# Channel mixes of the full final steps placed later in the following step, and the second row block's cast placed earlier

## The chip, the cores and the metric

The kernel runs on one core of a Trainium2 chip. The metric is the device time of one launch in microseconds (us), median of several runs; the kernel before takes 1473.58 us (six runs, 1470.38 to 1484.61). TensorE (PE) multiplies matrices into PSUM; VectorE (DVE) and ScalarE (ACT) read PSUM and work elementwise; GpSimd (POOL) adds in SBUF and issues part of the DMAs; SyncE (SP) only issues DMAs. Every engine works through its own instructions in order and waits on semaphores for the others.

## The reference

```python
# _attn_ref: a causal 7-tap filter per head along the sequence
w = softmax(weight)                            # 8 heads x 7 taps
x = out.reshape(B, S, D)                       # (8, 4224, 192), sum of 7 shifted rows
# _moe_ref
theta = x @ w_theta
zr, zi = x * cos(theta), x * sin(theta)
yr = einsum('ts,bsd->btd', w_tok_r, zr)        # 4224 x 4224 token mix
yi = einsum('ts,bsd->btd', w_tok_i, zi)
u = x + yr + yi
return u + maximum(u @ w_ch, 0.0)              # channel mix
```

Nearly all the work is the two token mixes, with matrices of 4224 x 4224 each applied to 8 x 192 = 1536 columns. After them each row of u goes through a 192 x 192 channel mix, is clipped at zero and added to u.

## The kernel before, in words

The 4224 tokens are cut into 33 chunks of 128 on the side that is summed over, and 33 row blocks of 128 on the output side. A chunk's filtered x, its cosine and sine products and their sums and differences are the seven planes of a `z` tile; at most 11 chunks are in SBUF at a time (`NW`). Output row blocks are visited in pairs, 17 visits to a round, and chunks come and go in a rolling manner, so that the whole run is 58 steps (`NSTEP`). Each step (`class Step`) takes a pair of row blocks through all chunks that are active, and adds the result to the partial sums of these rows, which live in DRAM (`part`) between visits. The tiles with the partial sums are called `pv`, two to a step, of 128 x 1536 float32.

A step of a pair has seven runs (`runs`), each over the n active chunks with two matmuls of 128 x 384 for each chunk (`mix`, L427): products of the two row blocks are shared so that seven runs do the work of eight. After a run `give` evicts an accumulator: DVE adds it to `pv` (L392). With n = 11, a full step, that is 154 matmuls.

The steps t = 41 to 57 are final: their rows are complete after them. Those from 41 to 52 have 11 chunks and a pair of rows; these are the "full final steps" that the change touches. From t = 53 (`late`) n falls to 9, 7, 6, 4 and 2, and their outputs go another way, with transposes on TensorE (`turn_u`).

For each of the two row blocks i of a full final step, `outputs` (L474) schedules this:

- `cast(i, g)` for g = 0, 1: ACT makes a float16 copy `ub` of half of `pv` (L449).
- `cross_u(i)`: ACT issues a DMA that transposes `ub` through the crossbar into `uT` (L155); `uT` has two buffers.
- `output(i, g)` for g = 0, 1: TensorE multiplies `uT` by the channel weights `wch` in 8 matmuls (`channel_mix`, L138), DVE clips and adds in one instruction (L464), and SP writes 384 KB to DRAM (L469).

The order of the work is written out by hand. Each of these tasks has a due time in us after the end of its own step, on a clock where a matmul counts 0.324 us per chunk and run (`self.time`, 24.95 for a full step). `step_events` turns the due time into a position in the following step, from 0 to 7 runs:

```python
found.append((7 * begin / steps[t].time, f))
```

and `mix` emits the task ahead of the first chunk whose place, run r plus c/n, has reached that position. TensorE, DVE, ACT and POOL then execute in the order of emission (`in_order`); for SP's DMAs the tile framework decides. Other tasks of a step that share these queues: `w_tasks` (DVE turns and sums the next step's weight tiles, L327 and L339), `load_w` (POOL loads weights into `st`, L314), `load_rows` (SP loads the next step's `pv`, L363; six buffers, and the transfer waits for the output transfers of the buffer's last user), and `add_x` (L370), which adds x to the partial sums of rows that have not had it. `add_x` has two forms. POOL adds an `xr` tile, which SP loads (L373 and L374); or, for late steps and four steps ahead, POOL issues DMAs that accumulate x into `part` in DRAM (L379), which happens in the steps from t = 49 on.

Of the kernel before, what the change touches and what calls it, by code (L numbers as in the profile page):

```python
# [16 lines left out]
def kernel(  # L17
# [262 lines left out]
    class Step:  # L280
# [193 lines left out]
        def outputs(self):  # L474

            found = []
            for i in range(len(self.tbs)):
                if not self.late:
                    at = (4 if i else 0.9 - self.time / 7) if self.pair else 0.7
                    for g in range(NG):  # L480
                        found.append((at + g, lambda i=i, g=g: self.cast(i, g)))
                        found.append((at + 10.5 + 2.8 * g,
                                      lambda i=i, g=g: self.output(i, g)))
                    found.append((at + 2, lambda i=i: self.cross_u(i)))
                    continue
                at = 1.2 if i or not self.pair else 0.6 - self.time / 7
                every, turn, mix = 2.0, 1.2, 3.6
                for g in range(NG):
                    found.append((at, lambda i=i, g=g: self.cast(i, g)))
                    found.append((at + turn, lambda i=i, g=g: self.turn_u(i, g)))  # L490
                    found.append((at + mix, lambda i=i, g=g: self.output(i, g)))
                    at += every
            return found
# [202 lines left out]
    for at, f in sorted(outputs, key=lambda e: e[0]):  # L696
        if at >= sum(s.time for s in steps):
            f()
# [28 lines left out]
```

## Time and profile before

| what | us |
|---|---|
| median of six runs | 1473.58 |
| lowest, highest | 1470.38, 1484.61 |
| the profiled execution | 1476.82 |
| its span, first to last instruction | 1475.0 |
| PE busy | 1419.9 (96%) |
| DVE busy | 1015.4 (69%) |
| POOL busy | 435.7 (30%) |
| ACT busy | 323.1 (22%) |
| crossbar transfers uT<-ub, 24 of them: issue to landing, least, median, most | 3.2, 6.9, 29.5 |

How to read it: the rows of the trace name the line, engine and operation, then what is written and read (`v<-wch,uT` reads `wch` and `uT` and writes `v`). In the rows of waits stand total time, count and the longest. In the chain and the time line the first two numbers are start and duration. An `x8` counts merged instructions. In rows of a window stand the busy times of PE, weight loads (PEld), DVE, ACT and POOL with counts, the clock that TensorE was granted, the share of the DMA engines, and GB/s.

### The profile page before, as it was taken

What the parts mean: (1) busy time and instruction counts of PE and PEld (TensorE: products, weight loads), DVE (VectorE), ACT (ScalarE), POOL (GpSimd) and SP (SyncE); (2) the same over time, 40 slices, a digit from 0 to 9 for tenths busy, and PEclk for the clock granted to TensorE, in tenths of its full rate; (3) what the DMA queues carried; (4) which work ended last, traced back from release to release, by engine and by line L of the source; (5) the groups of instructions that cost most, each with busy time, mean ns of one, the idle gap of its engine ahead of it and who ended that gap; (6) DMA issues with size and microseconds to landing.
All of it is one profiled execution on the core that took longest, in us unless ns stands there. A gap on an engine that the chain in (4) does not pass through costs nothing.

```text
span 1475.0 us, 23773 instructions
## 1 busy us (share of the span) xinstructions
PE 1419.9 (96%) x9807; PEld 886.9 (60%) x9807; DVE 1015.4 (69%) x1050; ACT 323.1 (22%) x413; POOL 435.7 (30%) x655
## 2 busy tenths in 40 slices
PE   7889999999999999999999999999999999995997
PEld 4556666666666666666656566666666666663665
DVE  6884554555458687777767758769787786773675
ACT  6861111111134353000000005245001001000034
POOL 7422211111223322522413333342133133333210
PEclk9999999999999999999999999999999999997999
DMA  9976756464699999997978799999889989999983
GB/s 178 223 162 145 143 100 147 95 151 89 157 223 221 221 215 270 193 241 172 243 168 210 173 196 238 192 238 263 154 199 212 210 196 234 197 272 140 225 220 119
DMA packets 272028, 281.98 MB, mean 191 GB/s; under 512 B 106672, under 2 KB 240176, under 8 KB 271920
## 3 DMA queue, kind: packets, MB, share of 16 engines
q0 software_dynamic: 162464, 92.15, 47.7%
q1 hardware_dynamic: 71824, 178.88, 34.9%
q10 hardware_dynamic: 37632, 9.44, 5.0%
q8 instruction: 77, 1.26, 0.3%
q14 instruction: 31, 0.25, 0.1%
HBM read 245.49 MB, written 108.13 MB: 240 GB/s over the span
## 4 chain that ended last, share of the span: by engine, by line
PE 85%; DVE 6%; DMA 4%; ACT 3%; issue 1%; POOL 0%; DVEq 0%; ACTq 0%; SPq 0%
PE y L427 77%; PE v L138 5%; DMA uT<-ub 3%; PE pc L200 2%; DVE pv L392 1%; ACT z L240 1%; PE tp L160 1%; DVE wt L339 1%; DVE wt L327 1%; DVE z L251 1%; DVE z L245 1%; ACT uT L148 1%; DVE pv L464 1%; DMA xw<-xw 1%; ACT pv L390 0%
## 5 line engine op out<-in xcount | busy, mean ns | idle before, releaser
L427 PE MATMUL y<-z,wt 128*128 128x384 f16 x7656 | 1291.5, 327 | 12.2 <-DVE pv L392 11.2
L427 PEld LDWEIGHTS <-wt 128*128 128x128 f16 x7656 | 740.5, 98 | 488.1 <-issue 14.7
L392 DVE TENSOR_TENSOR pv<-y,pv 128x768 f32<-128x768 f32 x324 | 308.5, 953 | 311.3 <-PE y L427 271.8
L327 DVE STREAM_TRANSPOSE wt<-st 128x1408 f16<-128x1408 f16 (+7 forms) x224 | 327.7, 1465 | 40.0 <-PE y L427 36.2
L314 POOL DMA_DIRECT2D st<-in_moe_w_tok_i_dram x232 | 132.7, 579 | 509.0 <-DVE wt L327 494.6
L314 POOL DMA_DIRECT2D st<-in_moe_w_tok_r_dram x232 | 132.8, 579 | 453.8 <-DVE wt L327 440.5
L339 DVE TENSOR_TENSOR wt<-wt 128x1408 f16<-128x1408 f16 (+7 forms) x216 | 217.3, 1006 | 45.7 <-PE y L427 43.7
L148 ACT ACTIVATE z<-pc 128x768 f16<-128x768 f32 x65 | 52.9, 813 | 389.6 <-PE pc L200 389.6
L449 ACT ACTIVATE ub<-pv 128x768 f16<-128x768 f32 x66 | 52.5, 836 | 361.7 <-DVE pv L392 350.8
L138 PEld LDWEIGHTS <-uT 128*128 128x128 f16 x1056 | 91.5, 98 | 41.9 <-DMA uT<-ub 18.4
L390 ACT ACTIVATE pv<-y 128x768 f32<-128x768 f32 x66 | 53.7, 813 | 282.7 <-PE y L427 282.7
L464 DVE SCALAR_TENSOR_TENSOR pv<-v,pv 128x768 f32<-128x768 f32 x66 | 62.6, 951 | 34.1 <-PE v L138 32.2
L187 POOL DMA_DIRECT2D xw<-in_x_dram x132 | 76.3, 584 | 30.5 <-DMA xw<-xw 7.5
L374 POOL TENSOR_TENSOR pv<-pv,xr 128x1536 f32<-128x1536 f32 x24 | 74.7, 3113 | 10.1 <-issue 8.8
L148 ACT ACTIVATE uT<-tp 128x768 f16<-128x768 f16 x79 | 63.0, 815 | 63.0 <-PE tp L160 62.1
L251 DVE TENSOR_TENSOR z<-z 128x768 f16<-128x768 f16 x132 | 73.3, 556 | 3.8
L138 PE MATMUL v<-wch,uT 128*128 128x192 f16 x528 | 54.9, 248 | 18.7 <-DMA uT<-ub 16.8
L240 ACT ACTIVATE z<-v,half_pi 128x768 f16<-128x768 f32 x66 | 59.6, 902 | 42.9 <-PE v L138 42.7
L245 DVE TENSOR_TENSOR z<-z 128x1536 f16<-128x1536 f16 x66 | 60.3, 949 | 9.9 <-ACT z L240 9.9
L138 PE MATMUL v<-wth,uT 128*128 128x192 f16 x528 | 55.0, 248 | 3.0 <-ACT z L240 2.8
L240 ACT ACTIVATE z<-v 128x768 f16<-128x768 f32 x66 | 53.1, 805 | 0.0
L160 PE MATMUL tp<-ident,z 128*128 128x128 f16 x396 | 33.0, 220 | 8.5 <-ACT z L240 8.0
(43 smaller groups left out, 146.8 us busy)
## 6 DMA issues: line engine op xcount, KB each, us to landing
part<-pv SPq DMA_DIRECT2D x79, 768.0 KB, 4.1
pv<-part SPq DMA_DIRECT2D x79, 768.0 KB, 5.8
out_dram<-pv SPq DMA_DIRECT2D x66, 384.0 KB, 5.3
st<-in_moe_w_tok_r_dram POOLq DMA_DIRECT2D x136, 176.0 KB, 5.2
st<-in_moe_w_tok_i_dram POOLq DMA_DIRECT2D x136, 176.0 KB, 5.2
xs<-z SPq DMA_DIRECT2D x132, 96.0 KB, 4.6
xw<-in_x_dram POOLq DMA_DIRECT2D x121, 96.0 KB, 6.0
xr<-xs SPq DMA_DIRECT2D x24, 384.0 KB, 4.5
```

Of the source, the lines that this page charges most:

```text
L138: pe(nc.tensor.matmul(v[:, k, b * D : (b + 1) * D], lhsT=tT[:, 3 * k + b + i, :], rhs=w[:, 2 * b + i, :], start=(i == 0), stop=(i == 1),))
L148: act(nc.scalar.activation(out=out, in_=in_, func=AT.Copy))
L187: nc.gpsimd.dma_start(out=self.xw[lo : lo + n, h, :, :], in_=x[:, t0 : t0 + n, :].rearrange("b s d -> s b d"),)
L240: act(nc.scalar.activation(**args))
L245: dve(nc.vector.tensor_tensor(out=o, in0=xv, in1=o, op=ALU.mult))
L251: dve(nc.vector.tensor_tensor(out=z[:, o, :], in0=z[:, a, :], in1=z[:, b, :], op=ALU.subtract))
L314: pool(nc.gpsimd.dma_start(out=st[a * Q : (a + 1) * Q, 0:nb, :, 0:n] .rearrange("i r bt s -> i (r bt) s"), in_=w[self.tbs[0] * P : (self.t ...
L327: dve(nc.vector.transpose(self.w[name][:, 0 : self.n, :, :], self.st[int(name[1])][:, int(name[0]) - 1, :, 0 : self.n * Q] .rearrange("p b ...
L339: dve(nc.vector.tensor_tensor(out=self.w[name][:, 0 : self.n, :, :], in0=self.w[a][:, 0 : self.n, :, :], in1=self.w[b][:, 0 : self.n, :, : ...
L392: dve(nc.vector.tensor_tensor(out=o, in0=yv, in1=o, op=ALU.add))
L427: pe(nc.tensor.matmul(y[cn][:, q, 0:BH], lhsT=self.w[wn][:, c, :, :].rearrange("p bt i -> p (bt i)"), rhs=chunks[k].z[:, zn, q * BH : (q + ...
L464: dve(nc.vector.scalar_tensor_tensor(out=ub, in0=channel_mix(self.uT[i][:, 6 * g : 6 * g + 6, :], wch), scalar=0.0, in1=ub, op0=ALU.max, o ...
```

## The change

Three due times in `outputs` change, for full final steps alone. The casts of the second row block (i = 1) are due 1 and 2 us after the step's end instead of 4 and 5, and its crossing at 3 instead of 6. The first row block's casts and crossing keep theirs (-2.66, -1.66 and -0.66). The four outputs no longer follow the casts by a fixed distance: they are due at 12, 14.7, 17.5 and 20.2 us after the step's end, instead of 7.84, 10.64, 14.5 and 17.3. What is computed stays the same, and each engine has the same instructions as before. On ACT and POOL their order stays the same as well; on PE, DVE and SP it changes.

```diff
             for i in range(len(self.tbs)):
                 if not self.late:
-                    at = (4 if i else 0.9 - self.time / 7) if self.pair else 0.7
+                    at = 1 if i or not self.pair else 0.9 - self.time / 7
                     for g in range(NG):
                         found.append((at + g, lambda i=i, g=g: self.cast(i, g)))
-                        found.append((at + 10.5 + 2.8 * g,
+                        found.append((12 + 5.5 * i + 2.7 * g,
                                       lambda i=i, g=g: self.output(i, g)))
                     found.append((at + 2, lambda i=i: self.cross_u(i)))
                     continue
```

## The prediction

> **What bounds the kernel now.** I read the page first (shares, chain), then TensorE's waits inside the full final steps, then the chain and the time line around the longest of them. Times are us of the one profiled execution.
>
> ```profile
> span 1475.0 us, 23773 instructions
> PE 1419.9 (96%) x9807; PEld 886.9 (60%) x9807; DVE 1015.4 (69%) x1050; ACT 323.1 (22%) x413; POOL 435.7 (30%) x655
> PE 85%; DVE 6%; DMA 4%; ACT 3%; issue 1%; POOL 0%; DVEq 0%; ACTq 0%; SPq 0%
> ```
>
> TensorE is busy 96% of the span, so 55 us of idle time is all that any reordering can win. The change touches t = 41 to 52, about 1050 to 1400 us, and there TensorE's waits are these:
>
> ```profile
> PE v L138 <- DMA uT<-ub: 16.8, 3, 14.8
> PE y L427 <- DVE pv L392: 0.7, 2, 0.4
> ```
>
> Three waits for a crossbar transfer (a "crossing") hold nearly everything, one of them 14.8 us. The chain of waits shows where each begins and how long its crossing was under way:
>
> ```profile
> 1276.38 10.26 DMA uT<-ub
> 1286.68 0.83 PE v L138 x8
> ...
> 1305.46 9.81 DMA uT<-ub
> 1315.31 0.83 PE v L138 x8
> ...
> 1334.09 23.77 DMA uT<-ub
> 1357.90 1.46 PE v L138 x8
> 1359.37 4.83 PE y L427 x16
> ```
>
> The second column is the duration. Each of the three is the first row block's crossing of a step (t = 49, 50, 51), wanted by the first channel mix of the next step. After the third, the eight channel-mix matmuls take 1.46 instead of 0.83 and the next 16 take 4.83 instead of 2.60 (that row elsewhere in the chain): the idle time also lowered the clock, for 0.6 + 2.2 = 2.9 us. What went on in the long wait:
>
> ```profile
> 1333.89 1.75 POOL L379 DMA_DIRECT2D part<-xs  x2
> 1334.09 1.32 ACTq L155 DMA_TRANSPOSE uT<-ub  x1
> 1337.33 0.34 SPq L363 DMA_DIRECT2D pv<-part  x1
> 1337.66 17.81 ACTq L155 DMA_TRANSPOSE uT<-ub  x1
> ```
> ```profile
> 1334.00:1343.00 9.00, 9.00 (x57) 5.28 (x54) 5.22 (x5) 1.63 (x3) 3.40 (x5) 1.00 1.30 220
> 1343.00:1358.00 15.00, 0.25 (x2) 0.10 (x2) 0.89 (x2) 0.00 (x0) 2.33 (x4) 0.62 1.25 72
> ```
>
> An accumulating transfer from POOL, the crossing and a partial-sum load from SP started together. The last three numbers of the lower rows are granted clock, DMA share and GB/s: while the DMA engines stay fully occupied (1.25), the rate falls from 220 to 72 GB/s and the clock to 0.62. In the steps before t = 49 there are no accumulating transfers, and no crossing was waited for.
>
> **The change, part by part.**
>
> *Channel mixes later.* A full step is 154 token matmuls of about 0.1625 us (96 in 15.60 in the chain). The emission positions 2.20, 2.985, 4.07 and 4.85 runs become 3.37, 4.12, 4.91 and 5.67, rounded up to the next of a run's 11 chunks: 50, 66, 90 and 108 matmuls ahead of the four mixes become 76, 92, 110 and 126. So they move by 26, 26, 20 and 18 matmuls: 4.2, 4.2, 3.25 and 2.9 us. Work is neither added nor removed. At t = 48 the first crossing was issued at 1248.72 and its mix began at 1257.57: 8.85 us of cover, which becomes 13.1. The second (1252.30 to 1265.39) had 13.1 and gets 16.3. If crossings land as they did:
> - waits of 1.29 (crossing 10.26) and 0.79 (9.81) go entirely: 2.1;
> - the 14.75 us wait shrinks by 4.2 to 10.5; it is still long enough to lose the clock, so the 2.9 stays;
> - the second crossing of that step was issued at 1337.66 and, at its 29.5 us (the longest landing of a crossing), landed at 1367.2. After a resume at 1357.9 come mix 1.46, 16 matmuls 4.83, mix 0.66, 18 matmuls 2.92, so the third mix wants it at 1367.8: just covered.
>
> *DVE.* Each moved output takes its 0.95 us DVE pass along. In steps where POOL adds x, S3 is held up (4.59 us at 1314.46 instead of 0.88, beside POOL's 3.12 us add at 1315.18), and in the chain an output pass and a 1.55 us weight turn then stood ahead of the eviction for which TensorE waited (the 0.7 above; about 0.3 more at 1098). Now the output pass leaves that place (-0.95) and TensorE arrives one mix (0.66) earlier: 0.29 better in each. I take 0.6 for all of them, between 0 and 1.0. Later in the step DVE has the passes that it no longer has earlier; every eviction has a whole run, 3.6 us, before its accumulator is written again, and I count at most two passes (1.9) ahead of one. Cost 0.
>
> *Second block's cast.* The order of ACT's instructions does not change, and neither does POOL's. ACT has nothing else in these steps: its waits there were
>
> ```profile
> ACT ub L449 <- DVE pv L392: 308.8, 20, 40.3
> ```
>
> so the cast starts when the eviction is done, wherever it stands. At 1332.48 and 1336.05 the two casts are already 3.57 us apart, one run, not the 6.66 of the old positions. Gain 0, from 0 to 0.3; its crossing does not start earlier either.
>
> *SP's queue.* A step's four output transfers stay four; each moves with its mix, and behind each pair of them stands a partial-sum load that waits for them to land (the buffer is theirs). So the loads come up to about 4 us later too; one load of x stands between two outputs now. The first load of a pair is over 30 us ahead of its use (issued at 1269.01, for the step that starts near 1306); the tightest I find, at 1408.49 for a step that starts near 1423 and wants it two runs in, has some 13. POOL's x add waits for such a load as well and has over 10. Cost 0, from 0 to 1.
>
> *Last full step.* t = 52's outputs run in a step of 9 chunks, where the last comes after the final matmul. Near the end TensorE has short waits for output passes (0.46, 0.43); one more DVE pass there costs 0 to 0.95; I take 0.3.
>
> Sum: 2.1 + 4.2 + 0.6 - 0.3 = 6.6 off this execution. It ran 1476.82 with a span of 1475.0 (1.8 around it) and is 3.2 above the median 1473.58. Without its crossing waits (16.8 + 2.9) it would have taken some 1457, and the fastest run shown is 1470.38, so every run seems to hold 13 us or more of them. Where they lie in more than one place, each place gives up to 4.2: from 6.6 (one long wait) to 13 (three). I take 8, nearer to the row that I have: 1473.6 - 8 = **1465.5**.
>
> [...] The crossings landed after 3.2 to 29.5 us, median 6.9. [...]
>
> **Rivals.**
> 1. *The long crossing does not come back* (0.22). The partial-sum load at 1337.33 sat between the two crossings; behind later outputs it moves to about 1341. If that load was what choked them, the whole 14.75 + 2.9 + 2.1 + 0.6 = 20.3 goes: 1476.8 - 20.3, about 1456. Against: the accumulating transfers and the crossing still start together, since both hang on DVE's order.
> 2. *Hidden or eaten* (0.15): later outputs lengthen the crossing by the 4.2 us given: 1473, with 1470 to 1478.
> 3. *Slower* (0.18): outputs and the first load of the pair now run right ahead of the crossing, in company with accumulating transfers. If the crossings at the ends of t = 49 and 50 take the 23.8 us that the one of t = 51 took, each costs 23.8 - 13.1 + 2.9 = 13.6, together 27 less the 6.6: about 1494; one alone gives 1480. It decides against the forecast once crossings pass 13.1 us by some 14 us in sum. For it: DMA shares there are already 1.0 to 1.3. Against: at the end of t = 50 a load (1302.60), two outputs and accumulating transfers did precede the crossing, and it took 9.81.
>
> **How the numbers follow.** My case has 0.45, on its own 1460 to 1470. About 0.5%, 7.4 us, is what a measurement of this kernel can tell from no change: below 1466.2 is faster. Of 0.45, I put 0.27 below it; with rival 1 that is 0.49. Same: 0.18 + 0.14 = 0.32. Slower: 0.19. The range reaches from rival 1's 1455 into the single extra long crossing, 1482, and leaves out half of rival 3 and the tail of rival 1.
>
> **What would show it.** Right: the waits for uT at the first mixes of t = 50 and 51 gone; one wait of about 10 us left at t = 52, after 76 matmuls of the step rather than 50; casts still one run apart; no wait for pv loads. Wrong: crossings over 13 us in other steps (rival 3), a crossing under 13 us at the end of t = 51 (rival 1), or the wait as long as before (rival 2).

## The result, and the profile after

The changed kernel takes 1462.92 us (median of 32 runs, 1455.8 to 1469.97), the kernel before 1474.24 us (69 runs, 1461.46 to 1490.18). The ratio is 0.9932, 95% interval 0.9918 to 0.9946: 0.68% faster, 10.0 us, between 8.0 and 12.1. The ratio is taken over the fast runs of both kernels, those within 1.5% of the kernel's fastest, so it is a little nearer to 1 than that of the two medians over all runs (11.3 us apart). The profiled execution of the changed kernel took 1468.74 us with a span of 1467.0, so it is one of the slower ones, 5.8 above the median.

These are the first lines of the page of the changed kernel, and TensorE's waits between 1040 and 1410 us, where the final full steps lie (total, times, longest):

```profile
span 1467.0 us, 23773 instructions
PE 1418.4 (97%) x9807; PEld 887.3 (60%) x9807; DVE 1016.7 (69%) x1050; ACT 323.1 (22%) x413; POOL 435.6 (30%) x655
```
```profile
PE v L138 <- DMA uT<-ub: 10.9, 3, 6.7
```

There are still three waits for a crossing, but 10.9 us in sum instead of 16.8, and the wait of matmuls for an eviction, 0.7 us before, is gone. The time line of TensorE shows where the three stand now (the bracket holds the idle time and what ended it):

```profile
1353.02 0.83 PE L138 MATMUL v<-wch,uT 128*128 128x192 f16 x8 [2.35 <-DMA uT<-ub]
1375.85 0.83 PE L138 MATMUL v<-wch,uT 128*128 128x192 f16 x8 [1.84 <-DMA uT<-ub]
1389.60 1.46 PE L138 MATMUL v<-wch,uT 128*128 128x192 f16 x8 [6.73 <-DMA uT<-ub]
```

None of them is one of the three places of before. The first is the third mix of t = 52, which wants the second row block's crossing; the other two are the first and third mixes of t = 53. The first mixes of t = 50, 51 and 52, which had waited 1.29, 0.79 and 14.75 us, now start without a wait. From the chain (start, duration, what):

```profile
1334.27 18.70 DMA uT<-ub
1353.02 0.83 PE v L138 x8
...
1360.78 5.97 ACTq L155
...
1368.47 21.08 DMA uT<-ub
1389.60 1.46 PE v L138 x8
```

and what the transfers of uT at the end of t = 51 took, from issue to landing, in the kernel before and then in the changed one (two transfers each):

```profile
DMA to landing us min/median/max: 23.8/26.6/29.5
```
```profile
DMA to landing us min/median/max: 10.0/14.3/18.7
```

What was issued around that place, from the time lines of POOL, ACT and SP, and how the DMA engines did in two stretches (last three numbers: granted clock, DMA share, GB/s):

```profile
1330.14 1.75 POOL L379 DMA_DIRECT2D part<-xs  x2
```
```profile
1330.54 2.02 ACTq L155 DMA_TRANSPOSE uT<-ub  x1
...
1334.27 5.51 ACTq L155 DMA_TRANSPOSE uT<-ub  x1
```
```profile
1336.34 0.34 SPq L363 DMA_DIRECT2D pv<-part  x1
```
```profile
1343.00:1353.00 10.00, 7.67 (x56) 4.94 (x53) 6.68 (x8) 0.00 (x0) 1.22 (x2) 1.00 1.21 142
...
1376.00:1389.60 13.60, 6.87 (x50) 4.42 (x49) 5.38 (x6) 0.84 (x1) 2.35 (x4) 0.89 1.28 207
```

Accumulation and the first crossing start together as before, but the load now follows both crossings; the DMA engines move 142 GB/s while the second one lags, where it had been 72. TensorE is busy for 7.67 of these 10 us, and keeps its clock (1.00, where it was 0.62 from 1343 to 1358 us before).

So two things differ: the mixes ask later, and at this place the crossings themselves were quicker. The experiments have to tell how much each is worth, and what makes a crossing late.

### The profile page after: what moved, and what is told of

It is laid out like the page before. It is cut to its first block, busy times and chain, and to the rows that moved or that the text cites. A ratio compares the mean times of both kernels' runs of the same rounds, so it can differ in the third digit from the quotient of the medians.

```text
span 1467.0 us, 23773 instructions
## 1 busy us (share of the span) xinstructions
PE 1418.4 (97%) x9807; PEld 887.3 (60%) x9807; DVE 1016.7 (69%) x1050; ACT 323.1 (22%) x413; POOL 435.6 (30%) x655
## 4 chain that ended last, share of the span: by engine, by line
PE 85%; DVE 5%; DMA 5%; ACT 3%; issue 1%; ACTq 1%; SPq 0%; DVEq 0%; POOL 0%
PE y L427 77%; PE v L138 5%; DMA uT<-ub 3%; PE pc L200 2%; DVE wt L339 2%; PE tp L160 1%; ACT z L240 1%; DVE pv L392 1%; DMA xs<-z 1%; ACTq L155 1%; DVE wt L327 1%; DMA pv<-part 1%; DVE pv L464 1%; ACT uT L148 0%; DVE z L245 0%
## 5 line engine op out<-in xcount | busy, mean ns | idle before, releaser
L427 PE MATMUL y<-z,wt 128*128 128x384 f16 x7656 | 1289.5, 326 | 11.6 <-DVE pv L392 10.5
L138 PEld LDWEIGHTS <-uT 128*128 128x128 f16 x1056 | 91.1, 98 | 35.5 <-DMA uT<-ub 12.1
L374 POOL TENSOR_TENSOR pv<-pv,xr 128x1536 f32<-128x1536 f32 x24 | 74.7, 3111 | 23.0 <-issue 11.1
L138 PE MATMUL v<-wch,uT 128*128 128x192 f16 x528 | 54.9, 248 | 12.8 <-DMA uT<-ub 10.9
```

The costliest lines, as they stand in the source:

```text
L138: pe(nc.tensor.matmul(v[:, k, b * D : (b + 1) * D], lhsT=tT[:, 3 * k + b + i, :], rhs=w[:, 2 * b + i, :], start=(i == 0), stop=(i == 1),))
L374: pool(nc.gpsimd.tensor_tensor(out=self.pv[i], in0=self.pv[i], in1=xr, op=ALU.add))
L427: pe(nc.tensor.matmul(y[cn][:, q, 0:BH], lhsT=self.w[wn][:, c, :, :].rearrange("p bt i -> p (bt i)"), rhs=chunks[k].z[:, zn, q * BH : (q + ...
```

## The experiments

The theory: the change gains by cover alone, since the mixes ask for a crossing 4.2 and about 3 us later; what makes crossings late in the last full steps is the accumulating DMAs that POOL issues beside them; the casts do nothing. The rivals: the earlier cast counts; or the outputs' and loads' new places on SP make the crossings themselves quicker or slower. Each comparison below is with runs of the kernel before on the same chip.

### The cast alone

```diff
-                    at = (4 if i else 0.9 - self.time / 7) if self.pair else 0.7
+                    at = 1 if i or not self.pair else 0.9 - self.time / 7
...
-                        found.append((at + 10.5 + 2.8 * g,
+                        found.append(((14.5 if i else 11.4 - self.time / 7) + 2.8 * g,
```

> The kernel before with the second block's cast and crossing due 3 us earlier, outputs as before. Theory (cover: only the later channel mixes matter, ACT casts as soon as the eviction is done): every engine keeps its order, ratio to before 1.000, time 1474, waits for uT of 13 to 20 us in the profile, casts 3.57 us apart as before. Rival (the earlier cast starts the second crossing earlier and spares the waits): ratio 0.993 like the full change.

Measured: 1477.19 us, ratio 1.0029 (0.9994 to 1.0063), no gain. The order of the instructions on PE, DVE, ACT, POOL and SP is that of the kernel before, so its profile is in effect a second one of that kernel. Its waits for uT sum to 20.7 us, six of them:

```profile
1123.06 1.46 PE L138 MATMUL v<-wch,uT 128*128 128x192 f16 x8 [3.55 <-DMA uT<-ub]
...
1365.33 1.46 PE L138 MATMUL v<-wch,uT 128*128 128x192 f16 x8 [13.18 <-DMA uT<-ub]
```

The long one is at the same place as before, the first mix of t = 52 (13.18; 14.75 before), after crossings of 22.2 and 27.4 us. So it came in both profiled executions of this order. Both are longer than their medians, and runs of the order go down to 1461.46 us, so it need not come in every run. The wait at 1123.06 is new, at a step without accumulating DMAs.

### The outputs alone

```diff
-                        found.append((at + 10.5 + 2.8 * g,
+                        found.append((12 + 5.5 * i + 2.7 * g,
```

> The kernel before with only the outputs due later (12, 14.7, 17.5, 20.2), casts as before. Theory (cover): all of the gain, ratio 0.993, 1463 to 1465. Rival (the cast carries part of it): 0.995 to 1.000. As this should execute like the changed kernel, its profile also tells how much crossings differ between two executions: by the theory the waits for uT stay under 12 us in sum.

Measured: 1462.9 us, ratio 0.994 (0.9907 to 0.9973): the whole gain. Every engine's order is that of the changed kernel. Three waits for uT sum to 7.8 us here, and the crossings at the end of t = 51 took 9.7 and 18.2 us (10.0 and 18.7 in the changed kernel's profile), so these too repeat.

### Without the accumulating DMAs, in both orders

```diff
-            for cols in (slice(0, HN), slice(HN, N)):
+            for cols in ():
                 pool(nc.gpsimd.dma_start(
```

> The kernel before without the DMAs that accumulate x into the partial sums of the late rows (these rows lack x). Theory (accumulating transfers beside the crossings make them late): crossings at the ends of t = 49 to 52 land within 9 us like those before t = 49, no wait for uT over 1 us, time 1474 less the some 17 to 20 us of waits, 1455 to 1458, ratio 0.988. Rival (the partial-sum load or the outputs beside a crossing make it late, accumulation or not): crossings of over 15 us stay, ratio above 0.995.

> The changed kernel without the same accumulating DMAs (the late rows lack x). Theory: no crossing is waited for in either order, so this is as fast as the kernel before without them, within 0.1% (the change is then worth only the 0.6 us of small DVE waits): 1455 to 1457. Rival (later outputs are worth 8 to 11 us in themselves, by other waits than those for crossings): 0.5 to 0.7% faster than the kernel before without them.

Measured: the kernel before without them 1459.09 us (1457.11 to 1460.4), ratio 0.992 (0.9885 to 0.9954); the changed kernel without them 1455.92 us (1454.85 to 1457.06), ratio 0.9905 (0.9876 to 0.9935). TensorE's waits in the old order, 1040 to 1410 us:

```profile
PE v L138 <- DMA uT<-ub: 1.1, 2, 0.7
PE y L427 <- DVE pv L392: 0.6, 2, 0.3
```

In the new order there is no row at all for that stretch. The ten crossings from 1249 us on, in the old order:

```profile
DMA to landing us min/median/max: 3.3/4.6/7.4
```

and the nine from 1251 us on in the new order:

```profile
DMA to landing us min/median/max: 5.2/6.6/11.0
```

(Both kernels leave out adding x to the rows of the steps from t = 53 on.) Without accumulation no crossing there takes over 11.0 us. The times of the old order lie within 3.3 us (7 runs), where those of the kernel before on the same chip lie within 34 (24 runs). Most of the change's value goes too: 3.2 us are left between the two orders (not the 0.1%, 1.5 us, that I had allowed). The two rows above account for 1.7 of them; the two profiled executions differ by 2.1 in span. So in these two orders the long crossings of the last full steps need the accumulating DMAs: up to 29.5 and 21.1 us with them, up to 7.4 and 11.0 without. That is shown. In these two executions the new order's crossings are some 2 us longer in the median, 6.6 against 4.6, with the outputs nearer to them; the 4 us of added cover more than make up for that.

### Accumulating DMAs kept, but issued 18 us ahead of the crossing

```diff
-                    found.append((3.3 + 1.7 * i, lambda s=s, i=i: s.add_x(i)))
+                    found.append((1.4 + 0.1 * i, lambda s=s, i=i: s.add_x(i)))
```

This is the line of `step_events` for rows with `ahead`. Once on the kernel before, once on the changed one:

> The kernel before with all accumulating DMAs of a step issued right after its first weight load (some 9 us into the step, about 18 ahead of the crossing) instead of half of them 0 to 5 us ahead of the crossing. Theory (it is being under way together that counts): crossings at the ends of t = 49 to 52 under 9 us as without accumulation, waits for uT about 1 us, 1457 to 1461, ratio 0.990. Rival (accumulation costs its traffic wherever it stands): ratio 0.996 or more, long crossings somewhere else in t = 49 to 53.

> The changed kernel with the same early accumulating DMAs. Theory: cover and calm crossings together, as without accumulation, 1455 to 1458, ratio 0.988 to 0.990, under both kernels. Rival: 1460 or more.

Measured: on the kernel before 1459.52 us, ratio 0.9929 (0.9903 to 0.9954), as much as the whole change under study; on the changed kernel 1456.52 us (1454.8 to 1457.9), ratio 0.9901 (0.9866 to 0.9935). In the second all six runs lie below 1458, as do 5 of the 32 runs of the changed kernel; the interval of its ratio overlaps that of the changed kernel, so how much it adds is not settled. The same bytes are accumulated; only the time differs: in the profiles the accumulating DMAs are issued 15 to 19 us ahead of the next crossing. Waits in the old order, 1040 to 1410 us, and its crossings from 1250 us on:

```profile
PE v L138 <- DMA uT<-ub: 1.9, 3, 0.8
PE y L427 <- DVE pv L392: 0.7, 2, 0.4
```
```profile
DMA to landing us min/median/max: 5.7/7.3/9.6
```

So it isn't the traffic as such, but when it is issued: up to 29.5 us for a crossing with accumulation issued beside it, up to 9.6 with it 15 to 19 us ahead.

### The late adds on POOL

```diff
-            self.ahead = self.late or 0 <= t + NU - NSTEP < 2
+            self.ahead = 0 <= t + NU - NSTEP < 2
```

> The changed kernel with x added to the late rows by POOL in SBUF one step ahead (one load of x on SP and a 3.1 us POOL add for each row block) in place of the accumulating DMAs. Theory (accumulation beside crossings is the cost): waits for uT under 1 us as without them, 1456; on top 0 to 6 us for DVE sums held up by POOL's adds in the short late steps: 1456 to 1462, ratio 0.988 to 0.992. Rival (any 384 KB of extra traffic there is as bad): waits of some 10 us stay, 1463 or more.

Measured: 1458.32 us (1456.07 to 1460.41), ratio 0.9883 (0.9836 to 0.993). No wait for uT shows in the profile. A plain load of 384 KB (an `xr` tile) is issued 0.4 us ahead of the first crossing at the end of t = 51, in the place of the accumulating transfers, and the two crossings take 8.0 and 9.5 us. The run was on another chip than those without accumulation or with early accumulation, and the intervals of the ratios (0.9905 and 0.9901 there) overlap with this one: which of the three is quickest, and what POOL's adds cost, is not shown.

### The outputs later still

```diff
-                        found.append((12 + 5.5 * i + 2.7 * g,
+                        found.append((16 + 4.2 * i + 2.1 * g if self.t < 52 else 12 + 5.5 * i + 2.7 * g,
```

> The changed kernel with the outputs of t = 41 to 51 due later again, at 16, 18.1, 20.2 and 22.3 us (those of t = 52 stay). Theory (cover): first mixes have about 17 us of cover, third ones about 19; the wait for the second crossing at the end of t = 51 (18.7 us in the changed kernel's profile) goes, those after t = 52 (crossings of 15 to 22 us) stay, so 1459 to 1462, ratio 0.990 to 0.992, 1 to 3 us under the changed kernel. Rival (outputs moved onto the crossings lengthen them): as slow as or slower than the changed kernel, 1463 to 1470.

Measured: 1457.08 us (six runs, 1455.27 to 1471.41), ratio 0.9894 (0.9839 to 0.995). Four of the six lie within 1455.27 to 1457.72, near the time without accumulation (taken on another chip). That fits more cover gaining more, but the loads behind the outputs move as well, and the interval overlaps that of the changed kernel. The profiled execution is the one at 1471.41, and there theory and rival both show: its crossings at the end of t = 51 took 20.3 and 28.5 us, with two outputs issued 1.8 and 2.3 us after the first crossing, and cover of 17 us still left waits of 2.54 and 5.01.

### One row block at a time

```diff
-                        found.append((at + 10.5 + 2.8 * g,
+                        found.append(((14.5 + 2.8 * g if i else 12 + 2.7 * g),
```

> The kernel before with only the first block's outputs later (12 and 14.7); the second block's stay at 14.5 and 17.3. Theory (cover; crossings of 18 to 29 us late in the final steps): the waits at first mixes go or shrink by 4.2 each, but the third mix, with 13 us of cover, waits for the second crossing by some 3 us more than in the changed kernel: ratio 0.995 to 0.997. Rival (the first crossing is the only one that matters): 0.993, as the full change.

```diff
-                        found.append((at + 10.5 + 2.8 * g,
+                        found.append(((17.5 + 2.7 * g if i else 11.4 - self.time / 7 + 2.8 * g),
```

> The kernel before with only the second block's outputs later (17.5 and 20.2); the first block's stay at 7.84 and 10.64. Theory (cover): the waits at first mixes stay whole, as they were all of the 16.8 us in the profile before: ratio 0.999 to 1.001, 1473. Rival (later transfers of the outputs, behind which the partial-sum load waits, are what shortens crossings): at least half of the gain, 0.996 or less.

Measured: the first block alone 1465.06 us, ratio 0.9929 (0.9891 to 0.9966); the second alone 1467.44 us, ratio 0.9945 (0.9914 to 0.9977). For the first, theory and rival lie within the interval. In its profile the wait has moved where the theory wanted it, to the third mix of t = 52, with crossings of 10.3 and 19.6 us:

```profile
1356.34 1.46 PE L138 MATMUL v<-wch,uT 128*128 128x192 f16 x8 [7.02 <-DMA uT<-ub]
```

The second is a clear miss of the theory: the first mixes have their old cover of 8.85 us, and yet 0.55% is gained. Its profile says how. The partial-sum load of SP and the accumulating DMAs, and the crossings of ACT, at the end of t = 51:

```profile
1340.14 1.76 POOL L379 DMA_DIRECT2D part<-xs  x2
```
```profile
1347.93 0.34 SPq L363 DMA_DIRECT2D pv<-part  x1
```
```profile
1340.79 1.71 ACTq L155 DMA_TRANSPOSE uT<-ub  x1
...
1344.36 5.29 ACTq L155 DMA_TRANSPOSE uT<-ub  x1
```
```profile
DMA to landing us min/median/max: 9.6/10.4/11.1
```

Accumulation is again issued together with the first crossing, but both crossings land within 11.1 us instead of 22 to 30. What differs most is the load: it waits for the second block's outputs to land, these come later (the last 2.5 us ahead of the first crossing, 5.0 in the kernel before), and so it is issued 7.1 us after the first crossing, behind both, and not 3.2 us after it, between them. Put in that order, six profiles with the accumulation issued within 0.9 us of the first crossing read (load after first crossing: landing of the two crossings, us):

| kernel | load after | first | second |
|---|---|---|---|
| the cast alone | 2.7 | 22.2 | 27.4 |
| before | 3.2 | 23.8 | 29.5 |
| first block alone | 3.6 | 10.3 | 19.6 |
| outputs alone | 5.3 | 9.7 | 18.2 |
| changed | 5.8 | 10.0 | 18.7 |
| second block alone | 7.1 | 9.6 | 11.1 |

Each row is one execution. Two more profiles have the accumulation 1.1 to 1.8 us ahead of that crossing: the outputs later still (load after 1.4, crossings of 20.3 and 28.5) fits the order, the loads in the order of emission below (load after 2.4, 14.7 and 23.5) does not quite. A load soon after the crossing goes with the longest ones here; that it makes them is not shown.

In this profile 4.09 of the 6.5 us of waits stand at t = 48, behind crossings of 11.8 and 15.8 us in a step without accumulation.

### The loads moved by themselves

Two runs that put SP's partial-sum loads elsewhere and leave the outputs. In both, SP is held to the order of emission for outputs and, from t = 42 on, for these loads, through `sp`, a helper like `pool`; in the first, made from the kernel before, `load_rows` is due behind the first block's outputs, in the second, made from the changed kernel, at its old place.

```diff
+    def sp(ins):
+        return in_order("sp", ins)
...
-                    nc.sync.dma_start(
+                    put = sp if self.t > 41 else (lambda ins: ins)
+                    put(nc.sync.dma_start(
                         out=pv, in_=part[(self.t // NU - 1) % 2][tb, :, :]
...
-            nc.sync.dma_start(
+            sp(nc.sync.dma_start(
                 out=out[g * GB : (g + 1) * GB, rows, :].rearrange("b s d -> s b d"),
...
-            found.append((1.6, steps[t + 1].load_rows))
+            found.append((3.25 if 41 <= t < 53 else 1.6, steps[t + 1].load_rows))
```

(The last pair is the first run's; the second keeps 1.6.)

> The kernel before (outputs at their old times) with both partial-sum loads of the next step held behind the first block's two outputs on SP (about 13 us into the step), so that no such load is near a crossing; accumulating DMAs stay. Theory (a crossing gets slow where an accumulating transfer and a partial-sum load are under way with it): the crossings at the end of t = 51 take 10 to 12 us instead of 22 to 29, waits for uT sum to 2 to 8 us, ratio 0.992 to 0.996. Rival (accumulating transfers suffice; the load does not matter and only the cover counts): the long crossing stays, ratio 0.999 to 1.001.

> The changed kernel with SP kept in the order of emission, so that both partial-sum loads of a step (1.5 MB) stand together behind the second block's outputs and run within some 3 to 8 us of the first crossing's issue, in every step. Theory (accumulation and a load beside the crossing): crossings at the ends of t = 49 to 52 of 15 to 30 us, waits for uT of 10 us and more, 1468 to 1480, so most of the change's gain lost though the cover is the same. Rival (cover alone): as the changed kernel, 1461 to 1465.

Measured: loads behind the first outputs 1474.85 us, ratio 1.0006 (0.9975 to 1.0036), no gain. By the letter the rival holds. But the run is not clean: POOL's x add of t = 51 waits for such a load, and the accumulating DMAs behind it slipped onto the crossing, issued 3.6 us before, 3.6 us after and 9.5 us after it; the crossings there took 15.1 and 23.2 us. In its profile, of one of its quicker executions (1468.13), the other ends of steps are calm (8.3 and 6.1 at t = 49, against 10.3 and 14.1 before). So crossings of 15.1 and 23.2 us came beside accumulation with no partial-sum load near (a load of x and an output were issued 3.5 and 3.1 us ahead of the first); what the load adds is left open.

Loads beside the crossing in every step: 1495.32 us (1479.97 to 1502.25), ratio 1.0135 (1.0078 to 1.0193), slower than both kernels by far, at the cover of the changed kernel. TensorE's waits, 1040 to 1410 us, then up to 1250 us alone, where nothing accumulates:

```profile
PE v L141 <- DMA uT<-ub: 28.9, 7, 12.2
```
```profile
PE v L141 <- DMA uT<-ub: 5.9, 2, 4.1
```

So crossings can be long beside ordinary loads too, up to 18.8 us before 1250, and with accumulation on top up to 26.5; most of the waiting, 23.0 of 28.9 us, lies where accumulation is on top. But a load close by does not suffice. Before 1250 the long ones are at the ends of t = 42, 46 and 47 (10.8 to 18.8 us), where one partial-sum load is issued 0.5 to 0.8 us after the first crossing and a load of x right behind it. At t = 43, 44 and 45, with loads 2.0 us ahead and 2.2 to 3.4 us after, the crossings took 5.7 to 7.2. And in the kernel before, at t = 46, with a load 0.7 us after and one of x 1.2 us after, they took 6.2 and 5.2. What decides between these is open.

## Why the prediction was right, and where it was not

Forecast was 1465.5, measured 1462.9; the size was 8 us and it was 10.0 (8.0 to 12.1). That the two are so near is in part luck. Of the signs that I had set down, two of the wrong ones came: the first crossing at the end of t = 51 took under 13 us, and those at the end of t = 52 took over 13. And I had raised the 6.6 of the sum to 8 because every run seemed to hold 13 us or more of such waits; that came from six runs, and of the 69 some go down to 1461.46, near the 1457 that I had worked out for none. Taken by its steps:

**Channel mixes later** held as worked out. In the changed kernel's time line the first mix of t = 49 starts at 1260.37, 13.1 us after its crossing was issued at 1247.29 (13.1 forecast); the third at 1267.21, 16.1 after 1251.15 (16.3). The waits of 1.29 and 0.79 us are gone.

**The long wait** is the step that failed in its place though not in its sum. I let the crossings land as they did, so that a wait of 10.5 us with a lost clock would be left at the first mix of t = 52. That crossing took 10.0 us and was covered. In its place the second block's crossing (18.7 us, cover 16) and the two at the end of t = 52 (15.0 and 21.1 us) were waited for, 10.9 us together. After the 6.73 us wait the mix took 1.46 us again instead of 0.82, at a granted clock of 0.50 (1389.6 to 1390.9 us; 1.00 from 1394 to 1400), so the lost clock stayed as well, in another place. A rough account of what cover is worth on the changed kernel's own crossings: with the old places of the mixes (8.85 us after the first crossing's issue, 16.7 for the third mix) its crossings would have cost 0.5 at t = 50, 1.1 and 4.6 at t = 52, 6.2 and 5.9 at t = 53, 18.3 in all; they cost 10.9, so cover is worth 7.4, near to the 6.3 that the old crossings gave in the forecast. The profile of the outputs alone, counted so, gives 18.0 against the 7.8 measured: 10.2 for cover. Counted so, the crossings of the old order's two profiles give 18.8 (before) and 21.3 (the cast alone). By this estimate the crossings of the new order were in sum little or no quicker, only long in other places, and cover is most of the gain. It holds each crossing fixed and rests on four executions, so the split is argued, not shown: the run with only the second block moved gained 0.55%, with a profile whose crossings at the end of t = 51 were quick, which my sum had not at all. Cover and quicker crossings overlap (0.9929 and 0.9945 for the halves, 0.9932 for both).

**DVE** held: the waits for evictions in these steps are gone (0.2 us is left in the profile of the outputs alone). **The cast** held: nothing (1.0029, interval from 0.9994), and in the changed kernel the casts of a step are 3.0 to 4.4 us apart, about one run, as before. The exceptions are 6.0 at t = 50 and 7.7 at t = 52 (5.8 and 5.1 before), where the profile puts the second cast's wait down to a turn of weights on DVE; I had read that the cast always starts with the eviction's end, and left out 7.7 us of such waits. **SP's queue** at "cost 0" was right as far as waits for loads go, and incomplete: I weighed only whether a load comes too late for its user. That it moves away from a crossing, or onto one, is what the change did to it; what that is worth in itself is not shown. **The last full step** cost 0 and not 0.3: without accumulation both orders show the same waits from 1365 us to the end of the kernel.

**Rivals.** The first (the load at 1337.33 chokes the crossing) holds in part: the long first crossing did not come back, and the load had moved from 3.2 to 5.8 us behind it; its alignment with accumulation, my reason against, was kept, and did not suffice to make the first crossing long. The second is there but small: without accumulation the later outputs go with crossings of 6.6 instead of 4.6 us in the median, less than the cover that they give. The third is a real danger, as the loads beside the crossing at 1.0135 show. At the end of t = 51 this change happens to move the load away. At the end of t = 52, where a load is issued 0.1 us and two outputs 0.5 and 1.0 us after the first crossing, the crossings took 15.0 and 21.1 us against 7.8 and 7.1 before, and 18.9 and 22.5 in the profile of the outputs alone. Set beside ordinary transfers of 384 KB in the kernel before, a crossing is not far off at the least, 3.2 us against 2.5 for an output and 2.8 for a load of x; in the median it is 6.9 against 5.3 and 4.5, and at the most 29.5 against 10.7 and 8.5.

What stays open: which part of the 10 us is cover and which quicker crossings; whether the load matters of itself beside accumulation, since the run that moved it alone moved the accumulation too; and why like neighbours leave a crossing short in one execution and long in another. At the end of t = 43, with a partial-sum load issued 0.5 or 0.6 us and a load of x 0.9 or 1.0 us after the first crossing, the two took 6.2 and 5.5 us in the old order without accumulation, and 12.6 and 16.6 with the cast alone.

## What to carry to other kernels

When an engine waits for a transfer whose time from issue to landing runs from 3 to 30 us, look first at what is issued within a few us of it; asking later hides the spread but leaves its cause: crossings of up to 21.1 us and waits of 10.9 remained in the changed kernel. Here, moving the accumulating DMAs 18 us ahead gave on the old order as much as the whole change, and on the new order a median of 1456.5 us (1462.9 without it, measured apart). And when a schedule moves a task, follow the transfers that wait behind it in their queue: where they land can matter as well (ratio 1.0135 with the loads beside the crossing in every step).

## What the runs showed of the hardware that I had not expected

In the kernel before, a crossing of 384 KB (`DMA_TRANSPOSE` in the trace) landed after 3.2 us where no other DMA was issued from 3.5 us ahead of it to 3.7 us behind it (1057.13), within 10 us in 20 of 24 cases, and after 29.5 us where accumulating DMAs and a partial-sum load were issued 3.8 and 0.3 us ahead of it; meanwhile, from 1343 to 1358 us, the DMA share stayed at 1.25 while the whole core moved 72 GB/s. Accumulation without a partial-sum load reached 23.2 us, loads and outputs without accumulation 20.5 (in the profile with the outputs later still, at t = 47). The spread of this kernel's executions goes with the accumulating DMAs: 1461 to 1490 us for the kernel before, 1457 to 1460 without them, in fewer runs. Nor did I expect that holding the loads next to the crossings could cost 1.35%, twice what the change under study gains.
